# Keys of batches 6 and 7 turned by DMA, with every fourth token in a run

## The chip, the core and the metric

The kernel runs on one core of a Trainium2 chip. Its time is the device time of one execution in microseconds (us), lower is better. Five engines work side by side, each through its own list of instructions in a fixed order, and wait for each other by semaphores: TensorE (PE: matmuls, with weight loads shown as PEld), VectorE (DVE), ScalarE (ACT), GpSimd (POOL) and SyncE (SP), which here issues nearly all DMAs. An instruction that waits holds up everything behind it on its own engine.

## What is computed

Eight batches of eight heads, 576 tokens, 64 values a head. Each token attends to 16 beacon keys and, causally, to the tokens up to itself; the result, 4608 rows of 512, goes through a feed-forward layer with a gate.

```python
k_all = np.concatenate([beacon_k, k], axis=2)          # 16 + 576 = 592 keys
v_all = np.concatenate([beacon_v, v], axis=2)
scores = scale * np.matmul(q, k_all.transpose(0, 1, 3, 2))
scores = np.where(causal, -1000000000.0, scores)
a = np.exp(scores - scores.max(-1, keepdims=True))
a /= a.sum(-1, keepdims=True) + 1e-09
attn = np.matmul(a, v_all)                             # (8, 8, 576, 64)
x = attn.transpose(0, 2, 1, 3).reshape(4608, 512)
out = (np.maximum(x @ w_gate, 0) * (x @ w_val)) @ w_out   # 512 -> 1536 -> 512
```

## The kernel before

**A plan made on the host.** The kernel's Python code first collects tasks (`add`): each has an engine or a choice of engines, an estimated cost, the tasks it depends on, the buffers it holds and a priority. `Plan.order` then goes through them in the order of estimated start times, gives buffers out, and writes the instructions down in that order. The order on each engine is therefore fixed when the program is built, but it comes out of estimates: a task with another estimate, another engine or another buffer moves its neighbours as well.

**Loading and turning queries and keys.** For scores, keys and queries must stand with the 64 values of a head on the partitions (`kT`, `qT`), two heads above each other. `load_pair` (L552) does this for 512 of a batch's tokens and two heads at a time, four times for keys and four times for queries, here called k0 to k3 and q0 to q3:

- an SP DMA loads 256 KB into a stage tile `st` (8 of them). Ordinarily each partition gets four tokens in a row of each of two heads, 1 KB a run (L563);
- a cast to bf16 into `h` (3 of them), on POOL from batch 2 on (L518);
- four 128x128 matmuls with the identity on PE turn it into PSUM (L529, `turned`);
- a copy on ACT or DVE moves it to `kT` or `qT` and undoes the order of four tokens to a partition (L467 and L469, the ACT and the DVE branch of `copy`).

For batch 7 (`TURN`) the last two steps are one DMA from SP that turns four 128x128 blocks (L574). So that the columns come out in order, the load then takes single tokens, in runs of 256 bytes and by two DMAs (L560).

The remaining 64 tokens and the 16 beacons go through `load_rest` (L610), called rest-K and rest-Q below, always with matmuls for the turn; values go through `load_v` (L647).

**Scores and softmax.** `quad_scores` (L727) makes scores for four heads at a time (g = 0 or 1) in three steps. A step has matmuls of up to 512 columns in a 64x64 quarter of the array, so four run together (L756). A score tile stays in PSUM, DVE adds the mask and takes the lowest value (L704, scores are negated), ACT takes the exponential into bf16 `pb` with the row sum (L711), DVE the reciprocal (L717), POOL multiplies (L722). The 16 last tokens of all heads of a batch have scores of their own (`last`, L797; matmuls at L806), here called F. Probabilities are turned by an SP DMA of 25 blocks (`pb` to `pTb`; 5 blocks for F, `pa` to `pTa`; L842), multiplied with values on PE (L852; F at L875) and copied to `xT`.

**Feed-forward.** `ffn` (L905) works on spans of up to 512 tokens: gate (L913) and value (L918) in 12 blocks of four 128x512 matmuls each, ACT and DVE for the gate and the product (L924, L929), and the output (L944) in rows of 128 tokens, evicted to `osb` and stored by SP (L958). It fills PE between the steps of attention.

**Order.** SP issues loads, turning DMAs and stores in one list. A turning DMA in that list waits for POOL, and what stands behind it waits as well. Turning DMAs of keys and queries have a priority that is 100 earlier than their load's (`TURN_FIRST`), those of probabilities 200 earlier (L843).

Of the kernel before, what the change touches and what calls it, by code (L numbers as in the profile page):

```python
# [12 lines left out]
ALU = mybir.AluOpType  # L13
# [21 lines left out]
ON_PE = 2  # L35
TURN = (7,)
TURN_FIRST = 100
# [27 lines left out]
AFTER = [[0.0, 12.0]]  # L65
PACE = 38.0


# [228 lines left out]
def kernel(  # L297
# [189 lines left out]


    def heads(src, b, s0, sl):
        return src[b, :, s0:s0 + sl, :].rearrange("h s d -> s h d")  # L490
# [6 lines left out]
    def new_batch(b, prio, work):  # L497
        t = Batch()
        t.b = b
        steps = 2 * sum(len(x) for x in (STEPS2 if b > BIGSTEP else STEPS if b >= SPLIT else STEPS_AB + STEPS_CDE)) + 1  # L500
        t.kT = Hold(kT_s, 2 * (NP + 1) + steps)
# [50 lines left out]
        def load_pair(kind, p, prio):  # L552

            src, s0 = {"k": (k, 0), "q": (q, 64 - Nb)}[kind]
            st = staged()

            def fetch(_):
                if b in TURN:
                    for i in range(2):
                        nc.sync.dma_start(st.tile.rearrange("p (n h d) -> p h n d", h=2, d=D)[:, i],  # L560
                                          src[b, 4 * (p // 2) + p % 2 + 2 * i, s0:s0 + MAIN, :].rearrange("(n p) d -> p n d", p=P))
                    return
                nc.sync.dma_start(st.tile.rearrange("p (h e) -> p h e", h=2),  # L563
                                  src[b, bass.ds(4 * (p // 2) + p % 2, 2, step=2), s0:s0 + MAIN, :].rearrange("h (p j) d -> p h (j d)", j=4))

            ld = add("DMA", (1.0, TURN_LOAD) if b in TURN else (0.5, 0.87), fetch, (held,), (st,), prio[0])
            dst = t.kT if kind == "k" else t.q
            h16, ca = rounded(dst, st, P, neg_scale if kind == "q" else 1.0, prio, ld,
                              lambda to, src: [(to, src)] if b in TURN else [(
                to.rearrange("p (j h d) -> p h j d", h=2, j=4), src.rearrange("p (h j d) -> p h j d", h=2, j=4))])  # L570
            zeros = on_zeros.get(b) if kind == "q" else None
            c0 = Nb if kind == "k" else 64
            if b in TURN:
                t.rows[kind, p] = [add("DMA", (1.22, 0.177 * 4), lambda _: nc.sync.dma_start_transpose(  # L574
                    dst.tile[:, p, c0:c0 + MAIN].rearrange("p (j n) -> p j n", j=4), h16.tile), (ca, zeros), (h16, dst), prio[0] - TURN_FIRST)]
# [7 lines left out]
            t.rows[kind, p] = [add(("ACT", "DVE"), {"ACT": c_act(512), "DVE": c_dve(512)}, evict, (tu, zeros), (ps, dst), prio[1])]  # L583

        def load_half(kind, g, half, prio):
# [24 lines left out]
        def load_rest(kind, prio):  # L610
# [21 lines left out]
            def evict(x):  # L632
                ps3 = ps.tile.rearrange("p (a n) -> p a n", a=NP)
                if kind == "k":
                    copy(x.engine, dst.tile[:, :, Nb + MAIN:], ps3[:, :, :REST])
# [26 lines left out]

        at, held = 0, None
        for what in ORDER0 if b == 0 else "KQ0011v2233vvvv":
# [15 lines left out]
    def softmax(t, parts, ph, prio, k):  # L680
# [3 lines left out]
        def view(i, lo=0):  # L684
            n, held, off = parts[i][:3]
            if len(held) == 1:
                return held[0].tile[:, off + lo:off + n]
            at = 512 * next(j for j, x in enumerate(bank) if x is held[0].tile)
            return psum[:, at + lo:at + n]

# [6 lines left out]
        for i, (n, held, _, msk, m, on, _, scored) in enumerate(parts):  # L697
            first = []
            if m < n:
                first = [add("DVE", c_max(n - m), lambda _, i=i, n=n, m=m: nc.vector.tensor_reduce(  # L700
                    out=at(7), in_=view(i)[:, :n - m], axis=AX.X, op=ALU.min), (scored,), held, prio + 0.001 * i + 0.0005 * k, 0.25)]

            def lowest(_, i=i, n=n, m=m, msk=msk):
                nc.vector.tensor_tensor_reduce(out=view(i, n - m), in0=view(i, n - m), in1=msk, scale=1.0,  # L704
                                               scalar=at(7) if m < n else 3.0e38,
                                               op0=ALU.add, op1=ALU.min, accum_out=at(i))

            lows.append(add("DVE", c_max(m), lowest, (scored, on, *first), held, prio + 0.001 * i + 0.0005 * k, 0.25))
        for i, (n, held, _, _, _, _, a, _) in enumerate(parts):
            def exp(_, i=i, n=n, a=a):  # L710
                nc.scalar.activation(ph.tile.rearrange("p a n -> p (a n)")[:, a:a + n], view(i), AF.Exp,  # L711
                                     bias=at(i), scale=-1.0, accum_out=at(4 + i))
# [14 lines left out]
    def quad_scores(t, g, step, phs, vals, prio, after):  # L727
# [23 lines left out]
        def scores(_):  # L751
            for j, lo, n, b_, off in cols:
                for i in range(2):
                    for k in ks:
                        r = slice(64 * k, 64 * k + 64)
                        nc.tensor.matmul(banks[k][b_].tile[64 * i:64 * i + 64, off:off + n],  # L756
                                         t.q.tile[r, 2 * g + i, 64 * j:64 * j + 64],
                                         t.kT.tile[r, 2 * g + i, lo:lo + n], start=True, stop=True)

# [16 lines left out]
    def quad(t, g, vals, prio, after):  # L776
# [4 lines left out]
        if PEQ(t.b, g):  # L781
            todo = list(range(NB_AB)) if ab else [i for i in range(21) if i not in (3, 7)] if t.b < SPLIT else list(range(NB))
            on_pe = [todo[i:i + 8] for i in range(0, len(todo), 8)]
        phs = [Hold(Slots([p_ab[t.b][:, 2 * g + k]]) if ab else p_s[1], max(1, len(on_pe))) for k in range(2)]
# [12 lines left out]
    def last(t, prio):  # L797
# [5 lines left out]
        def scores(_):  # L803
            for bank, a, n in ((sc[0], 0, 512), (sc[1], 512, SK - 512)):
                for pp in range(NP):
                    nc.tensor.matmul(bank.tile[32 * pp:32 * pp + 32, :n], t.q.tile[:, pp, S + Nb - TAIL:],  # L806
                                     t.kT.tile[:, pp, a:a + n], start=True, stop=True)
# [7 lines left out]
    def finish(t, p, vals, ph, pt_s, blocks, on_pe, outs, prio):  # L815

        pt = Hold(pt_s, len(vals) + max(1, len(on_pe)))
        if on_pe:
            tr = []
            for todo in on_pe:  # L820
                tp = Hold(first_ps if t.b == 0 else v_ps, 2)
                z = len(todo)
                runs = []
                for i, a in enumerate(todo):
                    if not runs or runs[-1][1] + runs[-1][2] != a:
                        runs.append([i, a, 0])
                    runs[-1][2] += 1

                def turn(_, todo=todo, tp=tp):
# [4 lines left out]
                def evict(x, runs=runs, tp=tp):  # L834
                    for i, a, n in runs:
                        copy(x.engine, pt.tile[:, a:a + n, :].rearrange("p a n -> p (a n)"), tp.tile.bitcast(BF16)[:, i * P:(i + n) * P])

                u = add("PE", 0.06 * z, turn, outs + [on_ident], (ph, tp), prio - 4)
                more = 0.07 * (len(runs) - 1)
                tr.append(add(("ACT", "DVE"), {"ACT": c_act(z * P) + more, "DVE": 0.08 + 0.0006 * z * P + more}, evict, (u,), (tp, pt), prio - 4))  # L840
        else:
# [131 lines left out]
    for b in range(B):  # L973
        batches.append(new_batch(b, {0: -20, 1: RANK1}.get(b, b * T0 - 8), b * T0 - AHEAD if b else -20))
    for b in range(B):
        for i, vals in enumerate([("AB", "CDE")] if b >= SPLIT else [("AB",), ("CDE",)]):
            for g in range(2):
                quad(batches[b], g, vals, b * T0 + (4 * g if b >= SPLIT else 4 * i + 2 * g) - (AB_FIRST if b < SPLIT and i == 0 else 0), AFTER[b][i] if b < SPLIT else PACE * (b + g / 2))
        last(batches[b], b * T0 + 8)
    for t in batches:  # L980
# [49 lines left out]
```

## Time and profile before

| | before |
|---|---|
| median of 3 runs | 402.75 us |
| the 3 runs | 403.11, 402.75, 399.99 us |
| the profiled execution | 399.48 us |
| its span | 397.8 us |
| PE busy | 386.6 us |
| DVE, ACT, POOL busy | 287.6, 261.7, 234.2 us |
| granted TensorE clock | 0.998 |

The span runs from the first to the last instruction of the profiled execution; 1.7 us of its time lie outside. The durations below come from that one execution, while the median comes from three others. [...]

### The profile page before, as it was taken

To read this page: it belongs to the slowest core of one execution; us is meant where nothing else is said; L and a number is where in the kernel's file an instruction comes from. 1 tells how busy PE (TensorE), PEld (TensorE's weight loads), DVE (VectorE), ACT (ScalarE), POOL (GpSimd) and SP (SyncE) were. 2 spreads that over 40 slices of the span, in tenths; PEclk is the share of its full clock that TensorE was granted. 3 is DMA by queue.
4 is the path that set the end of the run, shared out by engine and by line. 5 is a ranking of instruction groups with operands and counts; after the bars stand their busy time and mean duration, and the time that the engine had idled before them with its cause. 6 is when DMAs were issued, how large, how long until landed. Compare 5 with 4: busy or idle time off the path is not lost.

```text
span 397.8 us, 9897 instructions
## 1 busy us (share of the span) xinstructions
PE 386.6 (97%) x3235; PEld 203.8 (51%) x3278; DVE 287.6 (72%) x1024; ACT 261.7 (66%) x820; POOL 234.2 (59%) x454
## 2 busy tenths in 40 slices
PE   6999999999999999999999999999999999999995
PEld 4667855655454545455455445444454544444543
DVE  3999899788988697879697969687758733342432
ACT  2999699868967788668877878587737721320320
POOL 6899979849977576869669848646653520000000
PEclk9999999999999999999999999999999999999999
DMA  7999989999999799989999989798979184001102
GB/s 183 233 205 226 250 154 180 214 232 256 247 209 204 197 224 221 176 227 263 189 166 298 208 146 183 164 221 184 196 138 234 25 127 145 2 0 57 50 1 93
DMA packets 184100, 68.87 MB, mean 173 GB/s; under 512 B 158384, under 2 KB 179504, under 8 KB 184048
## 3 DMA queue, kind: packets, MB, share of 16 engines
q1 hardware_dynamic: 179216, 63.46, 73.7%
q0 software_dynamic: 4752, 4.72, 7.5%
q8 instruction: 25, 0.41, 0.5%
q14 instruction: 27, 0.22, 0.2%
q10 hardware_dynamic: 80, 0.07, 0.1%
HBM read 38.54 MB, written 9.44 MB: 121 GB/s over the span
## 4 chain that ended last, share of the span: by engine, by line
PE 88%; POOL 3%; DVE 3%; DMA 2%; issue 1%; SPq 1%; ACT 0%; POOLq 0%; ACTq 0%
PE f L918 23%; PE f L944 23%; PE f L913 22%; PE f L756 7%; PE f L852 6%; PE f L529 3%; DMA st<-in_q_dram 2%; POOL xT L722 2%; DVE f L704 2%; PE f L832 1%; PE f L996 1%; PE f L875 1%; PE f L806 1%; DVE osb L469 1%; POOL h L518 1%
## 5 line engine op out<-in xcount | busy, mean ns | idle before, releaser
L722 POOL TENSOR_SCALAR pb<-pb,small 128x448 bf16<-128x448 bf16 (+8 forms) x272 | 141.5, 539 | 70.5 <-DVE small L717 69.8
L711 ACT ACTIVATE pb<-f,small 128x320 bf16<-128x320 f32 (+8 forms) x272 | 143.9, 553 | 22.6 <-DVE small L704 17.7
L704 DVE CUSTOM_DVE_ANT_0 f<-f,mask 128x576 f32<-128x576 f32 (+8 forms) x288 | 133.7, 515 | 14.3 <-PE f L756 9.1
L918 PE MATMUL f<-xT,wv_r 128*128 128x512 bf16 (+3 forms) x467 | 107.3, 358 | 0.7
L913 PE MATMUL f<-xT,wg_r 128*128 128x512 bf16 (+3 forms) x468 | 105.4, 357 | 0.6
L929 DVE TENSOR_TENSOR hT<-g,f 128x512 bf16<-128x512 f32 (+3 forms) x120 | 75.4, 631 | 37.3 <-PE f L918 32.1
L944 PE MATMUL f<-wo_r,hT 128*128 128x512 bf16 (+3 forms) x438 | 99.6, 374 | 1.3 <-issue 0.5
L924 ACT ACTIVATE g<-f 128x512 f32<-128x512 f32 (+3 forms) x120 | 66.3, 562 | 50.9 <-PE f L913 44.2
L913 PEld LDWEIGHTS <-wg_r 128*128 128x128 bf16 x480 | 45.3, 98 | 43.7 <-issue 1.2
L918 PEld LDWEIGHTS <-wv_r 128*128 128x128 bf16 x480 | 43.4, 98 | 44.5 <-issue 5.2
L944 PEld LDWEIGHTS <-hT 128*128 128x128 bf16 (+2 forms) x456 | 42.1, 100 | 46.3 <-issue 2.1
L711 ACT ACTIVATION_READ_ACCUMULATOR pb<-f,small 128x1 f32 x272 | 60.9, 224 | 0.0
L518 POOL TENSOR_SCALAR h<-st 128x512 bf16<-128x512 f32 (+1 forms) x93 | 49.0, 541 | 11.0 <-DMA st<-in_q_dram 6.9
L469 DVE COPY osb<-f 128x512 f32<-128x512 f32 (+2 forms) x32 | 21.7, 682 | 28.1 <-PE f L944 27.7
L704 DVE DVE_READ_ACCUMULATOR2_ANT small<- 128x1 f32 x296 | 41.6, 141 | 0.0
L467 ACT CAST xT<-f 128x240 bf16<-128x240 f32 (+2 forms) x56 | 21.2, 385 | 30.7 <-PE f L852 29.5
L756 PE MATMUL f<-kT,qT 64*64 64x512 bf16 (+7 forms) x640 | 34.4, 295 | 0.1
L717 DVE RECIPROCAL small<-small 128x1 f32<-128x1 f32 (+3 forms) x136 | 20.9, 161 | 13.5 <-ACT pb L711 9.8
L529 PE MATMUL f<-ident,h 128*128 128x128 bf16 (+1 forms) x288 | 26.8, 222 | 1.6 <-POOL h L518 1.4
L529 PEld LDWEIGHTS <-h 128*128 128x128 bf16 (+1 forms) x288 | 20.0, 101 | 14.6 <-POOL h L518 4.0
L852 PE MATMUL f<-pTb,v 128*64 128x320 bf16 (+3 forms) x488 | 26.7, 253 | 0.0
L471 POOL TENSOR_SCALAR v<-st 128x512 bf16<-128x512 f32 (+1 forms) x38 | 23.2, 617 | 4.0 <-DMA st<-in_v_dram 4.0
(61 smaller groups left out, 217.5 us busy)
## 6 DMA issues: line engine op xcount, KB each, us to landing
out_dram<-osb SPq DMA_DIRECT2D x34, 256.0 KB, 2.4
st<-in_k_dram SPq DMA_DIRECT2D x28, 256.0 KB, 5.0
st<-in_q_dram SPq DMA_DIRECT2D x28, 256.0 KB, 5.1
st<-in_v_dram SPq DMA_DIRECT2D x24, 256.0 KB, 5.6
st<-in_k_dram SPq DMA_DIRECT2D x16, 128.0 KB, 4.2
st<-in_q_dram SPq DMA_DIRECT2D x16, 128.0 KB, 3.1
st<-in_v_dram SPq DMA_DIRECT2D x8, 224.0 KB, 5.2
wg_r<-in_moe_w_gate_dram POOLq DMA_DIRECT2D x3, 512.0 KB, 7.3
```

What stands on the lines that cost most here:

```text
L518: (nc.gpsimd if x.engine == "POOL" else nc.vector).tensor_scalar(to, src, by, 1.0, ALU.mult, ALU.mult)
L529: nc.tensor.matmul(to, h16.tile[:rows, a * P:(a + 1) * P], ident[:rows, :rows], start=True, stop=True)
L704: nc.vector.tensor_tensor_reduce(out=view(i, n - m), in0=view(i, n - m), in1=msk, scale=1.0, scalar=at(7) if m < n else 3.0e38, op0=ALU.ad ...
L711: nc.scalar.activation(ph.tile.rearrange("p a n -> p (a n)")[:, a:a + n], view(i), AF.Exp, bias=at(i), scale=-1.0, accum_out=at(4 + i))
L722: nc.gpsimd.tensor_scalar(one, one, at(8 + i), 1.0, ALU.mult, ALU.mult)
L756: nc.tensor.matmul(banks[k][b_].tile[64 * i:64 * i + 64, off:off + n], t.q.tile[r, 2 * g + i, 64 * j:64 * j + 64], t.kT.tile[r, 2 * g + i, ...
L852: nc.tensor.matmul(ps.tile[64 * hh:64 * hh + 64, d0:d0 + w], t.v.tile[:rows, c, D * h:D * h + D], rhs(64 * hh), start=(c == 0), stop=(c == ...
L913: nc.tensor.matmul(psg.tile[:, :mt], wg_r[:, ki, nf * P:(nf + 1) * P], xT[:, ki, m0:m0 + mt], start=(ki == 0), stop=(ki == KM - 1))
L918: nc.tensor.matmul(psv.tile[:, :mt], wv_r[:, ki, nf * P:(nf + 1) * P], xT[:, ki, m0:m0 + mt], start=(ki == 0), stop=(ki == KM - 1))
L924: r = add("ACT", c_act(mt), lambda _, psg=psg, g=g: nc.scalar.activation(g.tile[:, :mt], psg.tile[:, :mt], AF.Relu), (a,), (psg, g), -1000 ...
L929: hid.append(add("DVE", c_dve(mt), lambda _, psv=psv, g=g, nf=nf: nc.vector.tensor_mul(hT[nf].tile[:, :mt], g.tile[:, :mt], psv.tile[:, :m ...
L944: nc.tensor.matmul(ps[c].tile[64 * c:64 * c + rows, :w], hT[nf].tile[:, t0:t0 + rows], wo_r[:, nf, w * c:w * c + w], start=(nf == 0), stop ...
```

## The change

`TURN` becomes `KTURN = (6, 7)` for keys and `QTURN = (7,)` for queries.

- Keys of batch 6 are no longer turned by matmuls and copied, but by four DMAs.
- Keys of both batches are loaded in 1-KB runs of four tokens of a head. The turned blocks then hold every fourth token: `kT` stands in four runs j = 0..3 of 148 columns, run j with the tokens 4m + j, each run behind 12 columns that are left empty.
- Scores of these batches come out run by run: a matmul's moving operand is four pieces of a run each. The 512 and 64 columns of the last step become 432, 80 and 64. F takes 16 matmuls of 148 columns instead of 8 of 512 and 80.
- DVE reads the mask, and ACT writes the exponential, with a step of four elements, so that `pb` is in order again.
- `load_rest` writes keys by eight copies instead of two.

The diff, without the parts that the constants switch off (`QUADS = 9`, `PQUADS = 0`, lists of zeros):

```diff
-TURN = (7,)
+KTURN = (6, 7)
+QTURN = (7,)
...
+    RUN = 4
+    KW, KPAD = SK // RUN, 12
...
-    kT_s = Slots(many(2, [P, NP, SK], BF16, "kT"))
+    kT_s = Slots(many(2, [P, NP, RUN * (KPAD + KW)], BF16, "kT"))
...
+    def by_run(x):
+        return x.rearrange("p (j m) -> p j m", j=RUN)
+    def key_runs(x):
+        return by_run(x)[:, :, KPAD:]
+    def in_order(x):
+        return x.rearrange("p (m j) -> p j m", j=RUN)
...
-                if b in TURN:
+                if kind == 'q' and b in QTURN:
...
-            if b in TURN:
-                t.rows[kind, p] = [add("DMA", (1.22, 0.177 * 4), lambda _: nc.sync.dma_start_transpose(
-                    dst.tile[:, p, c0:c0 + MAIN].rearrange("p (j n) -> p j n", j=4), h16.tile), ...
+            if b in (KTURN if kind == "k" else QTURN):
+                to = (lambda: key_runs(dst.tile[:, p])[:, :, Nb // RUN:(Nb + MAIN) // RUN]) if kind == "k" else (
+                    lambda: dst.tile[:, p, c0:c0 + MAIN].rearrange("p (j n) -> p j n", j=4))
+                t.rows[kind, p] = [add("DMA", (1.22, 0.177 * 4), lambda _: nc.sync.dma_start_transpose(to(), h16.tile), ...
...
+                if kind == "k" and t.runs:
+                    for a in range(NP):
+                        for lo, n, at in ((Nb + MAIN, REST, 0), (0, Nb, REST)):
+                            copy(x.engine, key_runs(dst.tile[:, a])[:, :, lo // RUN:(lo + n) // RUN],
+                                 ps3[:, a, at:at + n].rearrange("p (m j) -> p j m", j=RUN))
...
+                own, against = view(i, n - m), msk
+                if t.runs:
+                    own, against = by_run(own) if m == n else view(i)[:, :, 512 // RUN:], in_order(msk)
...
+                to, x = ph.tile.rearrange("p a n -> p (a n)")[:, a:a + n], view(i)
+                if t.runs:
+                    to, x = in_order(to), by_run(x) if whole[i][0] != SK else x
...
-                        nc.tensor.matmul(banks[k][b_].tile[64 * i:64 * i + 64, off:off + n],
-                                         t.q.tile[r, 2 * g + i, 64 * j:64 * j + 64],
-                                         t.kT.tile[r, 2 * g + i, lo:lo + n], start=True, stop=True)
+                        keys = [(off, n, t.kT.tile[r, 2 * g + i, lo:lo + n])]
+                        if t.runs:
+                            runs = key_runs(t.kT.tile[r, 2 * g + i])
+                            w = 64 * (j + 1) // RUN
+                            keys = [(off, n, runs[:, :, :w])] if j < TILES else [(0, 3 * w, runs[:, :3, :w]), (3 * w, 512 - 3 * w, runs[:, 3, :512 - 3 * w])] if lo == 0 else [
+                                (off, n, runs[:, 3, w - n:w])]
+                        for at, w, x in keys:
+                            nc.tensor.matmul(banks[k][b_].tile[64 * i:64 * i + 64, at:at + w],
+                                             t.q.tile[r, 2 * g + i, 64 * j:64 * j + 64], x, start=True, stop=True)
...
-            for bank, a, n in ((sc[0], 0, 512), (sc[1], 512, SK - 512)):
+            for bank, at, a, n in ((sc[0], 0, 0, 512), (sc[1], 0, 512, SK - 512)) if not t.runs else [(sc[j // 2], 256 * (j % 2), (KPAD + KW) * j + KPAD, KW) for j in range(RUN)]:
```

More of the change, by code (lines that the diff above doesn't have):

```diff
@@ L583, in load_pair, with turned_pair, turn, evict @@
             t.rows[kind, p] = [add(("ACT", "DVE"), {"ACT": c_act(512), "DVE": c_dve(512)}, evict, (tu, zeros), (ps, dst), prio[1])]
+        def turned_pair(prio):
+            todo, waiting[:] = list(waiting), []
+            ps = [Hold(v_ps, 3) for _ in range(2)]
+            ps[0].next, ps[1].prev = ps[1], ps[0]
+            def turn(_):
+                for x, (_, _, h16, _, _, _) in enumerate(todo):
+                    for j in range(4):
+                        for r in range(2):
+                            for c in range(2):
+                                rows = slice(64 * r, 64 * r + 64)
+                                nc.tensor.matmul(ps[r].tile[64 * c:64 * c + 64, 256 * x + 64 * j:256 * x + 64 * j + 64],
+                                                 h16.tile[rows, j * P + 64 * c:j * P + 64 * c + 64], ident[rows, rows],
+                                                 start=True, stop=True)
+            tu = add("PE", 0.24, turn, [x[3] for x in todo] + [on_ident], (*[x[2] for x in todo], *ps), prio[1],
+                     part=2, lazy=TLAZY + LAZIES[b])
+            for x, (kind, dst, _, _, zeros, p) in enumerate(todo):
+                def evict(e, x=x, kind=kind, dst=dst, p=p):
+                    at = 512 * next(j for j, y in enumerate(bank) if y is ps[0].tile)
+                    c0 = Nb if kind == "k" else 64
+                    both = psum[:, at:at + 1024].rearrange("p (r y) -> p r y", r=2)[:, :, 256 * x:256 * x + 256]
+                    copy(e.engine, dst.tile[:, p, c0:c0 + MAIN].rearrange("p (r n j) -> p r n j", r=2, j=4),
+                         both.rearrange("p r (j n) -> p r n j", j=4))
+                t.rows[kind, p].append(add(("ACT", "DVE"), {"ACT": c_act(512), "DVE": c_dve(512)}, evict, (tu, zeros), (*ps, dst), prio[1]))
         def load_half(kind, g, half, prio):
@@ L688, in view @@
             at = 512 * next(j for j, x in enumerate(bank) if x is held[0].tile)
+            if t.runs and n == SK:
+                return by_run(psum[:, at:at + 1024])[:, :, :KW]
             return psum[:, at + lo:at + n]
@@ L819, in finish @@
             tr = []
+            quads = PQUADS and vals != ("F",)
             for todo in on_pe:
-                tp = Hold(first_ps if t.b == 0 else v_ps, 2)
                 z = len(todo)
+                tps = [Hold(first_ps if t.b == 0 else v_ps, 2) for _ in range(2 if quads else 1)]
+                if quads:
+                    tps[0].next, tps[1].prev = tps[1], tps[0]
+                tp = tps[0]
                 runs = []
@@ L827, in finish, with turn_quads @@
                     runs[-1][2] += 1
+                def turn_quads(_, todo=todo, tps=tps):
+                    for i, a in enumerate(todo):
+                        for k in range(2):
+                            for c in range(2):
+                                rows, cols = slice(64 * k, 64 * k + 64), slice(64 * c, 64 * c + 64)
+                                nc.tensor.transpose(tps[k].tile.bitcast(BF16)[cols, i * 64:i * 64 + 64], ph.tile[rows, a, cols], ident[rows, rows])
                 def turn(_, todo=todo, tp=tp):
@@ L973 @@
     for b in range(B):
-        batches.append(new_batch(b, {0: -20, 1: RANK1}.get(b, b * T0 - 8), b * T0 - AHEAD if b else -20))
+        batches.append(new_batch(b, {0: -20, 1: RANK1}.get(b, b * T0 - 8 + LOADS[b]), b * T0 - AHEAD if b else -20))
     for b in range(B):
```

52 lines of the change are left out of this document (37 added, 15 removed).

## The prediction

> **What bounds the kernel now.** I read the page first, then the windows of the stretch in which batches 6 and 7 are worked on, then PE's, SP's and POOL's timelines around the first place where the changed order differs.
>
> ```profile
> span 397.8 us, 9897 instructions
> PE 386.6 (97%) x3235; PEld 203.8 (51%) x3278; DVE 287.6 (72%) x1024; ACT 261.7 (66%) x820; POOL 234.2 (59%) x454
> PE   6999999999999999999999999999999999999995
> PE 88%; POOL 3%; DVE 3%; DMA 2%; issue 1%; SPq 1%; ACT 0%; POOLq 0%; ACTq 0%
> ```
> ```profile
> 240.00:280.00 40.00, 39.42 (x316) 19.02 (x321) 31.34 (x115) 30.77 (x106) 25.41 (x50) 1.00 0.93 188
> 280.00:320.00 40.00, 39.74 (x304) 18.93 (x307) 28.70 (x94) 26.66 (x84) 20.59 (x40) 1.00 0.70 141
> ```
>
> PE is the bound: 97% busy, every slice but the ends full, 88% of the chain. In the windows (columns PE, PEld, DVE, ACT, POOL, clock, DMA share) PE idles 0.6 and 0.3 us of 40. So there are no waits to win back: the time can only fall by PE work that disappears, and rises by each wait that PE meets. DVE has 60.0 of 80 us in this stretch, ACT 57.4, POOL 46.0. Full speed of PE is read from four 128x512 matmuls between two starts, 215.00 and 215.86 below: 0.216 us each.
>
> ```profile
> 211.53 1.57 PE L852 MATMUL f<-pTb,v 128*64 128x128 bf16 x32
> 213.04 1.90 PE L944 MATMUL f<-wo_r,hT 128*128 128x512 bf16 x7
> ...
> 214.78 0.39 PE L529 MATMUL f<-ident,h 128*128 128x128 bf16 x4
> 215.00 1.03 PE L944 MATMUL f<-wo_r,hT 128*128 128x512 bf16 x4
> 215.86 0.39 PE L529 MATMUL f<-ident,h 128*128 128x128 bf16 x4
> 216.18 0.63 PE L756 MATMUL f<-kT,qT 64*64 64x64 bf16 x16
> 216.75 0.40 PE L529 MATMUL f<-ident,h 128*128 128x128 bf16 x4
> ...
> 227.76 0.44 PE L806 MATMUL f<-kT,qT 128*32 128x512 bf16 x8
> 228.12 1.04 PE L918 MATMUL f<-xT,wv_r 128*128 128x512 bf16 x4
> ...
> 250.70 0.55 PE L756 MATMUL f<-kT,qT 64*64 64x512 bf16 x12
> 251.18 0.88 PE L852 MATMUL f<-pTb,v 128*64 128x128 bf16 x16
> ```
>
> **PE work removed.** Only batch 6 loses turns by matmul; keys of batch 7 went by DMA already. The changed instruction order has 68 groups of four turning matmuls where there were 72. A group takes 0.22 (214.78 to 215.00) to 0.32 us (215.86 to 216.18) of PE: 4 x 0.27 = -1.1 us. Bounds: -0.9, and -3.6 if each of 16 matmuls cost its whole length of 225 ns:
>
> ```profile
> L529 PE MATMUL f<-ident,h 128*128 128x128 bf16 x224 | 21.4, 225 | 1.5 <-POOL h L518 1.4
> ```
>
> The starts are 55 ns apart, so the lengths overlap, and the low end is the nearest. [...]
>
> **PE work added.** The last step of scores goes from 12 to 16 matmuls in two batches of two halves: 16 more, with the same columns. A step with 16 small matmuls takes 0.56 us (start 216.18 to the next turn at 216.75), 0.035 each: +0.5, bounds 0 (columns alone count) and 0.6. F goes from 8 matmuls to 16 in two batches; 8 take 0.36 us (227.76 to 228.12): +0.4, bounds 0 and 0.7. Moving operands in four pieces show nowhere; each piece is a contiguous run, so I put nothing on it. PE work in sum: -1.1 + 0.5 + 0.4 = -0.2 us, from -3.6 to +0.4.
>
> **DVE, ACT, POOL.** Four 512-column evictions go from ACT and DVE (-0.6 each, by the first row below). Rest-K is evicted by eight copies for two, in both batches:
>
> ```profile
> L467 ACT CAST kT<-f 128x512 bf16<-128x512 f32 x13 | 7.8, 601 | 9.4 <-PE f L529 9.4
> L467 ACT COPY osb<-f 128x512 f32<-128x512 f32 x4 | 2.4, 588 | 2.0 <-PE f L944 2.0
> L469 DVE CAST kT<-f 128x64 bf16<-128x64 f32 x6 | 1.3, 214 | 0.0
> L704 DVE CUSTOM_DVE_ANT_0 f<-f,mask 128x576 f32<-128x576 f32 x32 | 23.9, 773 | 5.3 <-PE f L756 2.6 <-POOL pb L722 2.5
> L704 DVE CUSTOM_DVE_ANT_0 f<-f,mask 128x128 f32<-128x128 f32 x32 | 9.2, 325 | 0.1
> L431 DVE TENSOR_REDUCE maskf<-xT 128x16 f32<-128x128 f32 x1 | 0.4, 368 | 2.4 <-POOL xT L426 2.4
> ```
>
> Eight of at most 214 ns are 1.7 us, under 1.2 more; it happens long before the first scores, beside engines with a quarter of their time free: nothing. Without that cover it is 1.2 us a batch. Steps of four elements: reading PSUM at a large step costs nothing (kT 601 against osb 588 ns). Reading SBUF with a step shows once: L431 reads 128 values 64 bytes apart and takes 368 ns, 43 more than a masked 128-column pass. That bounds the mask: (368 - 325) / 128 = 0.34 ns a column. A batch has 36 masked tiles, 11,520 columns: 0 to 3.9 us of DVE a batch, within its 20 us of idle time. A stepped ACT write shows nowhere; the same 0 to 0.34 ns bounds it by the nearest row. I take 0 on the path for both.
>
> **SP: where a wait can come from.** The four new turning DMAs take SP 1.2 us each and stand in its list ahead of other things, because their priority is 100 early. In the order before:
>
> ```profile
> 214.45 0.37 SPq L563 DMA_DIRECT2D st<-in_k_dram  x1
> 215.19 0.37 SPq L563 DMA_DIRECT2D st<-in_q_dram  x1
> 215.65 5.72 SPq L657 DMA_DIRECT2D st<-in_v_dram  x3
> 221.47 4.30 SPq L842 DMA_TRANSPOSE pTb<-pb  x1
> 226.97 5.29 SPq L842 DMA_TRANSPOSE pTb<-pb  x1
> 254.61 1.22 SPq L574 DMA_TRANSPOSE kT<-h  x1
> ```
> ```profile
> 213.47 2.46 POOL L518 TENSOR_SCALAR h<-st 128x512 bf16<-128x512 f32 x4
> 217.00 2.37 POOL L722 TENSOR_SCALAR pb<-pb,small 128x576 bf16<-128x576 bf16 x4
> 238.43 2.37 POOL L722 TENSOR_SCALAR pb<-pb,small 128x576 bf16<-128x576 bf16 x4 [2.55 <-DVE small L717]
> ```
> ```profile
> st<-in_q_dram SPq DMA_DIRECT2D x28, 256.0 KB, 5.1
> st<-in_q_dram SPq DMA_DIRECT2D x16, 128.0 KB, 3.1
> pTb<-pb SPq DMA_TRANSPOSE x28, 6.4
> kT<-h SPq DMA_TRANSPOSE x4, 3.2
> ```
> ```profile
> L563 SPq DMA_DIRECT2D st<-in_q_dram x4: 367/464/536, 208.1 to 215.2; - x4
> ...
> DMA to landing us min/median/max: 3.0/6.2/7.1
> ```
>
> The load of q3 of batch 6, at 215.19 before, now stands behind the turn of k0, both probability turns of batch 5's first half, and the turns of k1, k2, k3. Walk: k3's load ends at 214.8, k0's turn 216.1. The probability turn waits for POOL's four products, at 216.6 to 219 in the new order, and can start after two or three of them, at 218.5: to 222.8. Two stores, 1 us; the second turn, 4.3 to 5.3: 228.1 to 229.1. Three key turns with 1.3 between starts: 232 to 233. Then q3's load, landing 5.1 later (3.0 to 7.1): about 237.6; its cast takes 0.6: 238.2.
>
> PE gets there as follows. From 213.0 to the first scores of batch 6 the new order has 92 matmuls of 512 (19.9 us), three turns (0.7), three score steps (0.56, 0.56, 0.48) and 32 value matmuls (1.5): 236.7, with the scores 237.3. The next group on PE is q3's turn. PE waits 0.9 us, bounds 0 and 3.4. k1's turn, issued by 229.4 and landed 3.2 later at 232.6, is in time for those scores.
>
> On POOL q3's cast stands ahead of the four products that came at 238.43 before, so they start at 238.4 at best, and two probability turns follow them (with F's turn and a store) ahead of rest-Q of batch 7 on SP: 239.7 + 9.3 = 249, F's turn 250.7, rest-Q issued by 252.6, landed 3.1 later, cast 256.5. PE is at its turn after 64 matmuls of 512 (13.8 us) and 4 us of others, at 256.1: a wait of 0.4, bounds 0 and 2.5. The second of the two probability turns, started at 245 at the latest, lands 6.4 later at 251.4; PE wants it at 252.9. Batch 7's own key turns have 2.5 us or more to spare by the same walk, and its key loads become one DMA instead of two, which frees 0.5 us of SP each.
>
> **The sum.** -0.2 of PE work and +1.3 of waits: +1.1 us. The profiled execution has 399.48 us, a span of 397.8 and 1.7 around it: 400.6. The median shown is 402.75, so the same sum gives 403.9 there. The runs of one kernel lie at 399.5 to 400.0 and at 402.8 to 403.1; I take the middle, 402.3 us. One per cent (4 us) is about what a measurement of this kernel can tell from no change, as its three runs span 3.1 us.
>
> **Rivals.**
>
> Slower, by the list of SP (0.24). One mechanism: turns of keys that are far ahead of their use hold back loads that are needed at once. It decides if loads land at 7.1 us instead of 5.1: q3's turn then waits 2.9 us, POOL's four products behind the cast come 2 us later, both probability turns and rest-Q with them, and PE waits 2.4 there: 5.3 - 0.2 = +5.1, 404.6 by the profiled execution and 407.9 by the median. For it: loads at this place took 6.2 in the median, and DMA is 93% busy in the window that follows. Against it: fewer transfers share the time after 232, and batch 7 went through the same kind of turns without a wait on PE.
>
> Slower, by steps of four (0.12). If a stepped mask doubled the price of a column, (773 - 325) / 448 = 1.0 ns, DVE would get 11.5 us a batch more, 83 in a stretch of 80. It decides from about 0.7 ns a column, where DVE has 76 of 80, and costs 4 us (83 against 80 with nothing idle) to 12 (at 87% use): 404 to 412. For it stands only that no row shows 16 bytes between values; against it L431 with its 0.34 at 64 bytes. [...]
>
> Faster (0.09). Turns cost PE their lengths, -3.6, nothing is added and no wait comes: 395.9 by the profiled execution, 399.2 by the median, 0.9%; the lighter loads of batch 7's keys would have to take away some of what parts 400 from 403 as well. The starts 55 ns apart speak against it.
>
> That half of the change does nothing, since batch 7 turned its keys by DMA before, is certain by the order and lies in the forecast.
>
> **How the numbers follow.** The forecast, within 1%, has 0.55, the two slower rivals 0.24 and 0.12, faster 0.09. The likeliest case alone spans 399.3 (399.48 - 0.2, no wait) to 406 (402.75 with the bounds of the waits cut at 3). The range 399.0 to 408.0 takes in the first slower rival and the near half of the second, and leaves out the far ones.
>
> **What would show it right or wrong.** Right: 16 fewer matmuls at L529's line; PE idle of about 1 us by a wait of a turn for POOL's cast near 237 and another near 256; masked tiles and exponentials of batches 6 and 7 with the mean durations that they had. Wrong: waits of PE over 4 us between 230 and 300, a mean of a 576-column masked pass well above 773 ns, DVE near full in the two windows, or a span more than 2 us below 397.8.

## The result and the profile after

The changed kernel takes 420.29 us (median of 6 runs, 418.77 to 420.85), the kernel before 400.25 us beside it (median of 6, 399.49 to 403.11). The ratio is 1.0476, 95% interval 1.0435 to 1.0517: some 20 us slower, where the prediction said 402.3. The profiled execution has 420.85 us.

The head of the page, its chain (section 4 of the page), and the windows in which batches 6 and 7 are worked on (columns PE, PEld, DVE, ACT, POOL, clock, DMA share, GB/s):

```profile
span 418.2 us, 9971 instructions
PE 395.5 (95%) x3294; PEld 205.8 (49%) x3294; DVE 298.6 (71%) x1031; ACT 283.7 (68%) x821; POOL 234.0 (56%) x454
PE 68%; ACT 8%; DVE 7%; POOL 6%; issue 5%; DMA 4%; SPq 2%; POOLq 0%; ACTq 0%; DVEq 0%
```
```profile
240.00:280.00 40.00, 33.36 (x252) 15.20 (x251) 29.61 (x94) 31.52 (x77) 20.40 (x41) 1.00 0.85 174
280.00:320.00 40.00, 35.57 (x255) 16.82 (x255) 27.93 (x75) 27.02 (x64) 17.48 (x33) 0.91 0.63 130
320.00:340.00 20.00, 16.97 (x156) 8.79 (x155) 15.47 (x44) 16.20 (x41) 8.76 (x17) 1.00 0.39 76
```

PE idles 14.1 of these 100 us, where it idled 0.8 in the first 80 before. Yet DVE, ACT and POOL are not full: the fullest, ACT, has 16.2 of 20 us in the last window. An engine with time to spare can hold PE up all the same, and who does is in PE's waits from 236 us to the end and in the groups of ACT and DVE from 230 to 345 us:

```profile
PE f L832 <- ACT pb L780: 7.5, 7, 2.6
PE f L832 <- ACT g L1016: 2.1, 2, 1.3
```
```profile
L780 ACT ACTIVATE pb<-f,small 128x576 bf16<-128x576 f32 x10 | 13.1, 1376 | 6.2 <-DVE small L770 6.2
L770 DVE CUSTOM_DVE_ANT_1 f<-f,mask 128x576 f32<-128x576 f32 x8 | 9.4, 1206 | 0.0
```

A masked tile of 576 columns takes 1206 ns where it took 773. The mean of 1376 is over ten exponentials, two of them of batch 5; the eight of batches 6 and 7 take 1.54 us each, where before all took 738 ns. Over 576 columns that is 0.75 ns a column more on DVE and 1.39 on ACT.

Why this reaches PE shows where a group's third step of scores follows its second. PE and ACT, timelines:

```profile
247.52 5.35 PE L1036 MATMUL f<-wo_r,hT 128*128 128x512 bf16 x24
252.80 0.40 PE L832 MATMUL f<-kT,qT 64*64 64x432 bf16 x2
254.82 0.56 PE L832 MATMUL f<-kT,qT 64*64 64x432 bf16 x14 [1.61 <-ACT pb L780]
...
300.76 0.40 PE L832 MATMUL f<-kT,qT 64*64 64x432 bf16 x2
303.80 0.91 PE L832 MATMUL f<-kT,qT 64*64 64x432 bf16 x14 [2.63 <-ACT pb L780]
...
306.16 5.43 PE L1036 MATMUL f<-wo_r,hT 128*128 128x512 bf16 x16
311.52 0.88 PE L944 MATMUL f<-pTb,v 128*64 128x128 bf16 x16
```
```profile
252.17 1.41 ACT L780 ACTIVATE pb<-f,small 128x512 bf16<-128x512 f32 x1
...
253.34 1.42 ACT L780 ACTIVATE pb<-f,small 128x512 bf16<-128x512 f32 x1
```

The second step's scores stay in PSUM until masked and exponentiated, and 14 of the third step's 16 matmuls are released by the last of these exponentials. Between the two steps the order gives PE 24 matmuls of feed-forward, 5.28 us (247.52 to 252.80). That is all the time in which DVE and ACT can work unnoticed. The last exponential ends at 254.76 and PE goes on at 254.82. In batch 7 the same wait takes 2.63 us, and after it the 16 matmuls at 306.16 take 5.36 us, 0.335 each against the usual 0.216; the granted clock from 306.16 to 311.52 is given as 0.66.

### The profile page after: what moved, and what is told of

It is laid out like the page before. It is cut to its first block, busy times and chain, and to the rows that moved or that the text cites. A ratio compares the mean times of both kernels' runs of the same rounds, so it can differ in the third digit from the quotient of the medians.

```text
span 418.2 us, 9971 instructions
## 1 busy us (share of the span) xinstructions
PE 395.5 (95%) x3294; PEld 205.8 (49%) x3294; DVE 298.6 (71%) x1031; ACT 283.7 (68%) x821; POOL 234.0 (56%) x454
## 4 chain that ended last, share of the span: by engine, by line
PE 68%; ACT 8%; DVE 7%; POOL 6%; issue 5%; DMA 4%; SPq 2%; POOLq 0%; ACTq 0%; DVEq 0%
PE f L1005 17%; PE f L1036 17%; PE f L1010 17%; ACT pb L780 6%; PE f L832 6%; PE f L944 5%; DVE f L770 5%; PE f L550 3%; POOL pb L791 2%; POOL xT L791 2%; DMA st<-in_q_dram 1%; DMA pTb<-pb 1%; PE f L919 1%; DVE small L770 1%; POOL h L539 1%
## 5 line engine op out<-in xcount | busy, mean ns | idle before, releaser
L791 POOL TENSOR_SCALAR pb<-pb,small 128x320 bf16<-128x320 bf16 (+8 forms) x272 | 141.6, 539 | 96.9 <-DVE small L786 96.1
L780 ACT ACTIVATE pb<-f,small 128x448 bf16<-128x448 f32 (+8 forms) x272 | 168.0, 669 | 34.6 <-DVE small L770 29.3
L770 DVE CUSTOM_DVE_ANT_0 f<-f,mask 128x576 f32<-128x576 f32 (+8 forms) x216 | 100.3, 513 | 10.1 <-PE f L832 6.0
L1036 PE MATMUL f<-wo_r,hT 128*128 128x512 bf16 (+2 forms) x456 | 103.8, 379 | 0.0
L780 ACT ACTIVATION_READ_ACCUMULATOR pb<-f,small 128x1 f32 x272 | 64.4, 237 | 0.0
L770 DVE CUSTOM_DVE_ANT_1 f<-f,mask 128x64 f32<-128x64 f32 (+8 forms) x72 | 48.5, 737 | 0.8 <-PE f L832 0.6
L832 PE MATMUL f<-kT,qT 64*64 64x512 bf16 (+8 forms) x656 | 37.5, 293 | 10.7 <-ACT pb L780 7.5
L786 DVE RECIPROCAL small<-small 128x2 f32<-128x2 f32 (+3 forms) x136 | 20.9, 161 | 32.8 <-ACT pb L780 27.8
L832 PEld LDWEIGHTS <-qT 64*64 64x64 bf16 x656 | 15.6, 107 | 35.6 <-issue 31.2
L944 PEld LDWEIGHTS <-v 128*64 128x64 bf16 (+1 forms) x512 | 22.0, 111 | 9.8 <-issue 5.5
```

What stands on the lines that cost most here:

```text
L770: nc.vector.tensor_tensor_reduce(out=own, in0=own, in1=against, scale=1.0, scalar=at(7) if m < n else 3.0e38, op0=ALU.add, op1=ALU.min, ac ...
L780: nc.scalar.activation(to, x, AF.Exp, bias=at(i), scale=-1.0, accum_out=at(4 + i))
L791: nc.gpsimd.tensor_scalar(one, one, at(8 + i), 1.0, ALU.mult, ALU.mult)
L832: nc.tensor.matmul(banks[k][b_].tile[64 * i:64 * i + 64, at:at + w], t.q.tile[r, 2 * g + i, 64 * j:64 * j + 64], x, start=True, stop=True)
L944: nc.tensor.matmul(ps.tile[64 * hh:64 * hh + 64, d0:d0 + w], t.v.tile[:rows, c, D * h:D * h + D], rhs(64 * hh), start=(c == 0), stop=(c == ...
L1036: nc.tensor.matmul(ps[c].tile[64 * c:64 * c + rows, :w], hT[nf].tile[:, t0:t0 + rows], wo_r[:, nf, w * c:w * c + w], start=(nf == 0), stop ...
```

## The experiments

Ratios are to the kernel before, run beside each kernel on the same chip, with 95% intervals.

**Both steps moved, one at a time.** The same instructions in the same order on all engines, but one of the two walks its tile in token order: it reads (and for the mask writes) PSUM with the step, and SBUF in a row. First ACT alone:

```diff
                 if t.runs:
-                    to, x = in_order(to), by_run(x) if whole[i][0] != SK else x
+                    to = to.rearrange("p (m j) -> p m j", j=RUN)
+                    x = (by_run(x) if whole[i][0] != SK else x).rearrange("p j m -> p m j")
```

> The changed kernel, but ACT goes through a tile in the order of the tokens: it reads PSUM at a step of a run's length and writes the exponential without gaps. DVE's stepped mask stays. If ACT's stepped write (1537 ns for 576 columns after, 737 before) is the main cause: 576 columns back to about 740 ns, time 402 to 409. If the loss comes from the order of SP and PE or from the turns by DMA: 415 or more, with ACT back at 740 all the same. If it is the form of the access (four pieces), not the step on the SBUF side: ACT stays at about 1.5 us and the time at 420.

Measured: 403.63 us (402.59 to 404.48), ratio 1.0069 [1.0030, 1.0108]. The 576-column exponential is back at 737 ns, the masked pass still takes 1204. So ACT's step carries most of the loss. Then the mask alone, with ACT's step left in:

```diff
                 if t.runs:
-                    own, against = by_run(own) if m == n else view(i)[:, :, 512 // RUN:], in_order(msk)
+                    own = (by_run(own) if m == n else view(i)[:, :, 512 // RUN:]).rearrange("p j m -> p m j")
+                    against = msk.rearrange("p (m j) -> p m j", j=RUN)
```

> The changed kernel, but DVE goes through a tile in the order of the tokens: the mask is read without gaps, PSUM is read and written at a step. ACT's stepped write stays. If DVE's price (1206 ns for 576 columns after, 776 before) comes from the step on the SBUF side: back to about 780 ns; if from the form of the instruction: 1200 ns as before. If ACT is the main cause the time stays at 414 to 420; if DVE is, 402 to 409.

Measured: 415.54 us (413.11 to 417.97), ratio 1.0386 [1.0299, 1.0474]; exponential 1543 ns, masked pass 778. Then both edits together:

> Both of the above in one, so that only the DMA turns, the 1-KB runs, the PE work of the run order and the changed instruction order are left of the change. If the steps are the whole loss: 399 to 402, as the prediction's sum without its rivals has it, with PE's waits for ACT gone. If the order or the turns carry part of the loss: 405 or more, with waits of PE near 237 and 256 for a cast of POOL.

Measured: 399.48 us (397.76 to 401.72), ratio 0.9993 [0.9961, 1.0024]: the loss is gone, and nothing of the rest of the change can be seen in the time. PE meets no wait and is busy 40.00 of 40 us in both windows, of which the first is shown; then F's scores and the place that was shown above, and the last exponential there:

```profile
240.00:280.00 40.00, 40.00 (x344) 19.08 (x343) 30.58 (x116) 29.29 (x94) 26.02 (x51) 1.00 0.97 195
```
```profile
241.16 0.44 PE L884 MATMUL f<-kT,qT 128*32 128x148 bf16 x16
241.53 1.90 PE L1012 MATMUL f<-xT,wv_r 128*128 128x512 bf16 x8
...
251.94 0.57 PE L834 MATMUL f<-kT,qT 64*64 64x432 bf16 x16
252.44 1.57 PE L946 MATMUL f<-pTb,v 128*64 128x128 bf16 x32
```
```profile
250.65 0.71 ACT L782 ACTIVATE pb<-f,small 128x512 bf16<-128x512 f32 x1
```

The last exponential ends at 251.36, 0.58 us ahead of PE. The two single edits at the same place, first the one without ACT's step, then the one with it:

```profile
252.15 0.67 PE L833 MATMUL f<-kT,qT 64*64 64x432 bf16 x16
```
```profile
251.43 0.69 ACT L781 ACTIVATE pb<-f,small 128x512 bf16<-128x512 f32 x1
```
```profile
256.42 0.40 PE L833 MATMUL f<-kT,qT 64*64 64x432 bf16 x2
257.99 0.56 PE L833 MATMUL f<-kT,qT 64*64 64x432 bf16 x14 [1.16 <-ACT pb L781]
```

With the mask's step alone the last exponential ends at 252.12, 0.03 us before PE comes: the same 24 matmuls just cover it. With ACT's step alone PE waits. So the loss is not proportional to the work added: the step of the mask uses up the spare time here, that of the exponential goes past it.

**A cheaper step on ACT.** `both`, but the exponential (F's excepted) writes at every second column, 4 bytes apart, and reads PSUM in a row. This leaves the probabilities of batches 6 and 7 out of order.

```diff
-                    to = to.rearrange("p (m j) -> p m j", j=RUN)
-                    x = (by_run(x) if whole[i][0] != SK else x).rearrange("p j m -> p m j")
+                    if whole[i][0] != SK:
+                        to, x = to.rearrange("p (m j) -> p j m", j=2), x.rearrange("p (j m) -> p j m", j=2)
+                    else:
+                        to, x = to.rearrange("p (m j) -> p m j", j=RUN), x.rearrange("p j m -> p m j")
```

> The kernel without steps on the SBUF side, but ACT writes the exponential of batches 6 and 7 at every second column (F excepted; probabilities of these batches stand in a wrong order). The list of prices has 935 ns for 576 columns at that step, 190 more than without. If the loss grows in proportion to ACT's price (800 ns more made 15.5 us), 3 to 4.5 us more than without: 403 to 404.5. If the kernel has slack for a quarter more and only then loses: 399 to 401.

Measured: 400.33 us (398.09 to 403.55), ratio 1.0024 [0.9991, 1.0057]. The 512-column exponentials at this place take 0.85 instead of 0.70 us, the last ends 0.23 us ahead of PE, and PE is busy 40.00 of 40 us in both windows. Here a dearer exponential that stays under the cover costs nothing that the time shows.

**The steps without the rest.** The kernel before, with no change to loads, turns or `kT`; in batches 6 and 7 the mask is read and the exponential written with a step of four, which leaves their probabilities out of order.

```diff
+                if t.b > 5:
+                    own, against = own.rearrange("p (j m) -> p j m", j=4), msk.rearrange("p (m j) -> p j m", j=4)
...
+                if t.b > 5:
+                    to, x = to.rearrange("p (m j) -> p j m", j=4), x.rearrange("p (j m) -> p j m", j=4)
```

> The kernel before, with nothing but the two steps of four put on in batches 6 and 7 (mask read and exponential written at every fourth column; the probabilities of these batches stand in a wrong order). Instruction order as before. If the steps are the cause: 414 to 420. If the order or the turns are: 400 to 404.

Measured: 418.86 us (418.43 to 419.28), ratio 1.0469 [1.0415, 1.0523], the same as the whole change. PE's waits begin with

```profile
PE f L762 <- ACT pb L717: 5.5, 6, 1.6
```

This settles the cause from the other side: the steps alone are enough.

**What a step costs.** The kernel before, with steps of 2, 4, 8 and 16 in batches 2 to 5 in both places, and batch 6 with the step of four on the PSUM side.

> The kernel before, as a list of prices: exponential written and mask read at a step of 2 in batch 2, 4 in batch 3, 8 in batch 4, 16 in batch 5; in batch 6 instead PSUM is gone through at a step and SBUF without gaps (probabilities of batches 2 to 5 stand in a wrong order). [...] If any step costs the same: ACT 1.5 us for 576 columns and DVE 1.2 us at every step. Batch 6: as before, 740 and 775 ns, if PSUM's side is free.

Measured, one run: 480.78 us (400.54 before). The groups for 576 columns: ACT at no step, 2, 4, 8 and with the step on the PSUM side; DVE at no step, 2, 4, 16 and the PSUM side:

```profile
L726 ACT ACTIVATE pb<-f,small 128x576 bf16<-128x576 f32 x12 | 8.9, 746 | 1.6 <-DVE small L709 1.3 <-DVE small L741 0.2
L728 ACT ACTIVATE pb<-f,small 128x576 bf16<-128x576 f32 x4 | 3.7, 935 | 0.4 <-DVE small L711 0.4
L730 ACT ACTIVATE pb<-f,small 128x576 bf16<-128x576 f32 x4 | 5.7, 1540 | 2.4 <-DVE small L713 1.3 <-POOL h L518 1.1
L732 ACT ACTIVATE pb<-f,small 128x576 bf16<-128x576 f32 x4 | 10.8, 2934 | 2.9 <-DVE small L715 1.5 <-POOL h L518 1.4
L736 ACT ACTIVATE pb<-f,small 128x576 bf16<-128x576 f32 x4 | 2.9, 738 | 1.8 <-DVE small L719 1.8
```
```profile
L709 DVE CUSTOM_DVE_ANT_0 f<-f,mask 128x576 f32<-128x576 f32 x12 | 9.1, 768 | 1.6 <-PE f L780 0.9 <-POOL pb L746 0.4
L711 DVE CUSTOM_DVE_ANT_1 f<-f,mask 128x576 f32<-128x576 f32 x4 | 3.0, 770 | 0.0
L713 DVE CUSTOM_DVE_ANT_1 f<-f,mask 128x576 f32<-128x576 f32 x4 | 4.6, 1204 | 0.0
L717 DVE CUSTOM_DVE_ANT_1 f<-f,mask 128x576 f32<-128x576 f32 x4 | 4.3, 1128 | 0.0
L719 DVE CUSTOM_DVE_ANT_0 f<-f,mask 128x576 f32<-128x576 f32 x4 | 2.9, 778 | 0.7 <-POOL pb L746 0.7
```

At the steps left out above, DVE takes 1202 (8) and ACT 2743 (16). So no one price holds for every step. The mask's read is free with values 8 bytes apart (770 against 768), takes 1204 at 16, and no more beyond (1202 at 32, 1128 at 64). The exponential's write is dearer at smaller distances already: 935 against 746 at 4 bytes; at a step of four, 8 bytes, it takes 2.1 times as long (1540); at eight, 16 bytes, 3.9 times. A step of four on the PSUM side costs neither engine anything that can be seen (738 against 746, 778 against 768).

**Is it ACT, the exponential, or the write?** The kernel before; evictions walk their tiles in another order, to the same places. `kT` (2-byte values) is written at every fourth column.

```diff
+                if kind == "k":
+                    to, x_ = dst.tile[:, p, c0:c0 + MAIN].rearrange("p (n j) -> p j n", j=4), ps.tile.rearrange("p (j n) -> p j n", j=4)
...
                 copy(x.engine, dst.tile[:, p, c0:c0 + MAIN].rearrange("p (n j) -> p n j", j=4),
                      ps.tile.rearrange("p (j n) -> p n j", j=4))
```

> Is the dear stepped write a property of the write on ACT, of the exponential, or of any engine's write? The kernel before, with only the order in which evictions walk their tiles changed, the same values in the same places. The eviction to kT (128x512, bf16) writes at every fourth column, 8 bytes apart, and reads PSUM in a row, where before it was the other way round; the eviction to qT stays as it was, as a control. The eviction to osb (128x512, 4-byte values) writes at every second column (8 bytes apart) for the second 128 rows of a span and at every fourth (16 bytes) for the third; the first and fourth rows stay. Every second span's osb goes to ACT, the rest to ACT or DVE as planned. Theory 1, it is ACT's write, by the distance in bytes: ACT's kT goes from 601 ns to about 1300 (512 columns at 1.39 ns more), its osb from 588 to about 1300 at 8 bytes and about 2500 at 16 (the exponential's 2675 at 16 bytes less some); DVE's kT stays at 682, its osb at 690 at 8 bytes and rises at most to 1050 at 16. Theory 2, it is the exponential with its row sum alone: all copies on ACT stay within 5% of 601 and 588. Theory 3, it is SBUF's side and holds for every engine: DVE's kT rises to 1300 as well. Theory 4, on ACT it goes by the number of elements skipped and not by bytes: osb on ACT takes about 800 at every second (exponential at step 2: 920 against 723) and about 1300 at every fourth. The whole time says little: a dear kT delays scores of six batches, 400 to 430.

Measured, one run: 420.98 us. The `kT` groups at 8 bytes:

```profile
L585 DVE CAST kT<-f 128x512 bf16<-128x512 f32 x16 | 20.9, 1306 | 4.0 <-PE f L529 3.9
L583 ACT CAST kT<-f 128x512 bf16<-128x512 f32 x8 | 10.5, 1315 | 3.3 <-PE f L529 3.3
```

Theory 3: both engines pay the same (601 on ACT and 682 on DVE in a row), so it is the write into SBUF, neither ACT nor the exponential. `osb` at 16 bytes took 1085 on ACT and 1115 on DVE, one instruction each: less than `kT` at 8 bytes. That left distance against width of the value:

> The run before showed the dear stepped write on DVE too (1306 ns for 682 where 2-byte values lie 8 bytes apart) and cheaper for 4-byte values (1085 and 1115 ns at 16 bytes). Which is it, the distance in bytes or the width of the value? The kernel before; only the order in which evictions walk their tiles is changed, values and places are the same. The eviction to kT (128x512, bf16) writes at every second column (4 bytes) in batches 1 and 2, at every eighth (16 bytes) in 3 and 4, at every sixteenth (32 bytes) in 5 and 6. The eviction to osb (4-byte values) writes at every second column (8 bytes) in half of the feed-forward spans and at every fourth (16 bytes) in the other half, on ACT and on DVE in turn. Theory 1, the width: a 2-byte value that does not share its write with a neighbour costs more than a 4-byte one at the same distance; ACT's and DVE's kT take 2000 ns or more at 16 bytes, as ACT's exponential (2675), osb 1050 to 1150 at 16 and 590 to 700 at 8. Theory 2, distance alone: kT at 16 bytes takes about 1100 as osb does and kT at 8 bytes was the worst. Theory 3, DVE differs from ACT beyond 8 bytes: DVE's kT stays at 1300 at 16 and 32 bytes, as its masked pass stayed at 1200 from 16 bytes on, while ACT's rises to 2600. At 4 bytes all expect 680 to 900. The whole time says little, 410 to 450.

Measured, one run: 415.33 us (402.91 before). `kT` on ACT at 4 and 16 bytes and on DVE at 16, then `osb` on ACT at 8 and 16:

```profile
L584 ACT CAST kT<-f 128x512 bf16<-128x512 f32 x3 | 2.2, 747 | 0.0
L591 ACT CAST kT<-f 128x512 bf16<-128x512 f32 x4 | 9.8, 2457 | 2.8 <-PE f L529 2.8
L593 DVE CAST kT<-f 128x512 bf16<-128x512 f32 x4 | 9.8, 2439 | 1.4 <-PE f L529 1.4
L980 ACT COPY osb<-f 128x512 f32<-128x512 f32 x10 | 6.3, 626 | 8.6 <-PE f L966 8.0 <-ACT pb L733 0.7
L987 ACT COPY osb<-f 128x512 f32<-128x512 f32 x9 | 9.8, 1086 | 11.2 <-PE f L966 11.2
```

The width, theory 1. At 16 bytes a 4-byte value costs 2.1 ns (1086 / 512) and a 2-byte value 4.8 (2457 / 512); DVE's `osb` takes 691 at 8 bytes and 1079 at 16, like ACT's. The runs give times by distance and width alone; whether neighbours share a write they do not show.

**Telling the planner.** The changed kernel, with the measured durations as the plan's costs (0.3 + 0.00222 a column on ACT, 0.16 + 0.00183 on DVE).

> The changed kernel, but the plan is told what the stepped instructions take (ACT 0.3 us and 2.22 ns a column, DVE 0.16 us and 1.83 ns a column), so that it orders PE by them. The instructions are the same. If PE's waits come from an order that was made with too low prices: 404 to 412. If ACT and DVE are simply full: 415 or more.

A miss: 435.47 us (433.08 to 437.85), ratio 1.0873 [1.0718, 1.1029]. The plan put more feed-forward between the earlier steps and left PE none from 296.8 to 322.6 us, where the softmax of batch 7 stood exposed; one of PE's waits there:

```profile
317.29 1.55 PE L944 MATMUL f<-pTb,v 128*64 128x128 bf16 x16 [6.28 <-DMA pTb<-pb]
```

**Less and more turning by DMA.** `both` with `KTURN = (7,)`, then with `KTURN = (4, 5, 6, 7)`.

> The kernel without steps on the SBUF side, with only batch 7's keys in runs and turned by DMA (batch 6 turns by matmul, as before). It tells whether the four added turning DMAs cost anything: 399 to 402 if they do not; 2 us or more under the version with batch 6 as well if they do.

Measured: 400.49 us (399.66 to 403.19), ratio 0.9995 [0.9957, 1.0033]: the four turning DMAs of batch 6 are not seen in the time either way.

> The kernel without steps on the SBUF side, with the keys of batches 4 and 5 turned by DMA as well. By the sum of the prediction each batch gives PE 1.1 us and takes 0.45 for the split matmuls (halves of what two batches take): 1.3 us less than without, 397 to 400. If the turning DMAs hold back loads on SP where all engines are busier (batch 4 and 5): 402 or more, with waits of PE for POOL's casts.

A miss: 417.05 us (412.93 to 420.62), ratio 1.0359 [1.0296, 1.0422]. SP, POOL, PE's longest kind of wait, and PE where batch 7's last scores end:

```profile
297.79 1.59 SPq L581 DMA_DIRECT2D st<-in_q_dram  x2
```
```profile
302.55 0.62 POOL L539 TENSOR_SCALAR h<-st 128x512 bf16<-128x512 f32 x1 [15.05 <-DMA st<-in_q_dram]
```
```profile
PE f L946 <- DMA pTb<-pb: 11.4, 3, 9.1
```
```profile
332.52 0.57 PE L834 MATMUL f<-kT,qT 64*64 64x432 bf16 x16
...
335.21 1.02 PE L1038 MATMUL f<-wo_r,hT 128*128 128x512 bf16 x4
345.37 1.54 PE L946 MATMUL f<-pTb,v 128*64 128x128 bf16 x16 [9.13 <-DMA pTb<-pb]
```

A load of queries stands on SP behind two probability turns, three stores and two turns by DMA, goes out at 297.79, and POOL waits 15.05 us for it. But PE does not wait for POOL's casts: it is busy 40.00 of 40 us from 240 to 280 and from 280 to 320. It stops at 336 us, because between the last step of scores (332.52) and the values that need its probabilities the order has 8 feed-forward matmuls, where `both` has 72. So the cover had been used up earlier, as in `told`. Whether the late load or the plan's estimates for eight more turning DMAs made that order was not taken apart.

## Why the prediction was wrong, by its own steps

**The step that failed** is "a stepped ACT write shows nowhere; the same 0 to 0.34 ns bounds it by the nearest row. I take 0 on the path for both". The nearest row was a read, on DVE, of 4-byte values. The write of 2-byte values measured 1.39 ns a column, four times the upper bound, and the mask 0.75, twice. L431 was a poor stand-in even for the mask, for it set a reduction with one operand against a masked pass with two: at that row's 64 bytes the masked pass itself pays (1128 - 768) / 576 = 0.63. No row of before scatters single values in a write into SBUF, so nothing there bounded the price from above.

**The cover was mis-stated too.** "Within its 20 us of idle time" sets the price of one batch against DVE's idle time in a whole 80 us stretch, in which two batches are worked on. What counted was the 5.28 us between two score steps. With both steps free (`both`) 0.58 us are to spare there; in the change the last exponential ends 1.96 us late (254.76 against 252.80), so with the steps the same work ends some 2.5 us later. Neither engine came near the 76 of 80 us from which the steps-of-four rival was to decide: in the changed kernel DVE had 57.5 and ACT 58.5 of the 80 us from 240 on.

**That rival** (0.12) named steps of four, but the lesser of the two. Its price, 404 to 412, was too low because it charged DVE alone: with ACT left free the chip gives 403.6. Its sums were off as well: 83 against 80 is 3 us, not 4, and 83 us of work at 87% use take 95, which is 15 more than 80, not 12.

**Where the 21.4 us of span between `both` and the change lie.** From the first scores of batch 6 to the end the change takes 181.4 us (from 236.84) and `both` 159.1 (from 237.67), 22.2 more; up to there the change is 0.8 ahead. PE's idle time in this stretch is 14.8 us larger; its list of waits from 236 us on, those shown above and six smaller kinds, sums to 14.6 in 17 waits. PE's busy time is 7.4 us larger for the same matmuls. Of that, 2.9 lie behind the long wait of batch 7: from 303.80 to 311.52 the change takes 7.72 us for 14 score, 16 value and 16 feed-forward matmuls, and `both` some 4.8 for the same ones. The other 4.5 are 0.26 a wait: the matmul before a wait has its whole length counted, where others cost the distance to the next start (0.216 us of a length of 0.38 for 128x512), and at 252.80 to 254.82 this makes 2.02 us of a shown wait of 1.61 and two matmuls of 0.035, 0.34 more. That this holds for all 17 is an estimate from that place.

**PE's own work** came out some 0.7 us below the forecast, by other terms. `both` has 16 fewer turning matmuls, as foreseen. The last score step costs 0.50 us (251.94 to 252.44) against 0.48 before, not 0.12 to 0.14 more; F takes 0.37 (241.16 to 241.53) against 0.36. Both added terms, +0.5 and +0.4, should have been near 0.1 in sum: at these places four and eight more matmuls on the same columns cost 0.02 and 0.01 us. With -0.9 to -1.1 for the turns the change saves some 0.9 us of PE, where the forecast had 0.2, and the span of `both` is 1.0 under that of before, which its interval of 0.3% in the ratio neither shows nor excludes. So `both`, at 399.48 us, lies inside the range of 399.0 to 408.0, but not by the sum of the prediction: neither of the two waits in it (+1.3) came.

**SP's walk** was right in its times and wrong in its waits. SP and POOL of the changed kernel around q3's load:

```profile
232.35 0.57 SPq L584 DMA_DIRECT2D st<-in_q_dram  x1
```
```profile
235.76 0.62 POOL L539 TENSOR_SCALAR h<-st 128x512 bf16<-128x512 f32 x1 [1.97 <-DMA st<-in_q_dram]
```

The load goes out at 232.35 (walk: 232 to 233), and the first scores start at 236.84 (walk: 236.7). But the data is there 3.4 us after the issue, not 5.1, so the cast ends at 236.38 and the turn starts at 237.41 without a wait. Rest-Q's turn does not wait either, in the change or in `both`. The first slower rival (0.24) did not occur. With four batches turned a load does go out late, but PE meets no wait of that kind there.

## What to carry to other kernels

Where columns must be put in order between PSUM and SBUF, put the step on the PSUM side and walk SBUF in a row: here the step costs nothing there, 738 and 778 ns against 746 and 768, and 20 us on the other side. Weigh a slower instruction against the work that stands between it and the next use of its buffer (here 24 matmuls, 5.28 us), not against an engine's idle share: 0.15 us more on a 512-column exponential was swallowed whole, 0.7 more stopped PE. An operation that no row shows has no upper bound by a row of another kind; the forecast then has to carry a case in which it is dear.

## What the runs showed of the hardware that was not expected

By the evictions of `before`, `write_steps` and `write_widths`, a write into SBUF that scatters 2-byte values is dear on ACT and DVE alike: for 512 columns 601 to 682 ns in a row, 747 at 4 bytes (on ACT), 1306 to 1315 at 8, 2439 to 2457 at 16, and no more at 32 (2333 to 2361). Scattered 4-byte values cost nearly nothing at 8 bytes (626 and 691, against 588 and 690 in a row) and take 1079 to 1086 at 16. What in the memory makes a 2-byte value cost twice a 4-byte one was not shown.

In the changed kernel, after PE had idled 2.63 us, the granted clock was 0.50 from 303.80 to 306.16 and 0.66 from 306.16 to 311.52, where 16 matmuls took 0.335 us each; behind that it was 1.00. The 1.61 us of idling before 254.82 had no such effect: the clock is 1.00 from 252.80 to 260. But in `steps_alone`, where PE's longest wait for ACT is 1.6 us, the mean clock from 280 to 320 is 0.96, between 1.00 from 240 to 280 and 1.00 from 320 to 360. So by these runs the length of one wait does not decide it; what does was not tried.
